# Linear attention and four experts on one core: w1 of expert 0 in halves of F by two row blocks, layer 1 of tile 0 split at two head pairs, a new order of the first steps, last stores on three queues

## The chip, the cores and the metric

The kernel runs on one core of a Trainium2 chip. The metric is the device time of one execution in microseconds. Times are medians over several executions; the profile is of one further execution. In the profile PE is TensorE (matrix products), PEld its weight loads, DVE is VectorE, ACT is ScalarE, POOL is GpSimd, and SP is SyncE, which mostly issues DMAs. A "q" behind the name means the queue that issues, not the engine's arithmetic.

## What is computed

```python
def phi(x):
    return np.where(x > 0, x, np.exp(x) - 1.0) + 1.0
q_p, k_p = (phi(q), phi(k))                      # (8, 8, 576, 64): batch, heads, sequence, head size
kv = np.einsum('bhsd,bhse->bhde', k_p, v)
z = np.sum(k_p, axis=2)
num = np.einsum('bhsd,bhde->bhse', q_p, kv)
den = np.einsum('bhsd,bhd->bhs', q_p, z)[..., None] + 1e-06
attn = num / den
x = attn.transpose(0, 2, 1, 3).reshape(4608, 512)
p = domain_probs / (domain_probs.sum(-1, keepdims=True) + 1e-09)
for e in range(4):                               # w1: (4, 512, 1024), w2: (4, 1024, 512)
    out += p[:, e:e + 1] * (np.maximum(x @ w1[e], 0.0) @ w2[e])
```

All arrays are float32.

## The kernel before

**Tiles.** The 4608 tokens are nine tiles of 512. Tiles 0 to 7 are the first 512 tokens of each of the eight batches, and tile 8 gathers the last 64 tokens of all batches. For each batch the kernel makes phi(k), phi(q), the matrix kv with z as a 65th column, the numerators and denominators, and turns the normalized result into `xT` (features on partitions, tokens along the row). Then four experts follow, each with a layer 1 (`w1`), a ReLU and a layer 2 (`w2`). Products are in float16 with float32 sums in PSUM.

**Two forms of the experts.** In tile 0, expert 0 uses plain products in layer 1, and all four experts use plain products in layer 2 (`y`). All else uses seven products in place of eight on 2 x 2 blocks. The blocks' sums come from DVE (sums of weights, steps `s` for w1 and `t` for w2), from POOL (sums of tokens `ts`, except in tile 0, where DVE makes them, and sums of hidden values `hs`), and from copies on ACT between the products.

**The names of the steps.** The order list uses these names, and so do the change and the prediction:

- `lq0..3`, `lk0..3`, `lv0..3`: SP's loads of batch 0. `lq` i holds half i//2 of the tokens and heads 0 to 3 or 4 to 7 (i % 2); `lk` and `lv` i hold two heads each. `lpr0` and `lpr` load the probabilities.
- `ke`, `kl`, `km`: exponential, linear part and their minimum of k in batch 0. `qe`, `ql`, `qm`: the same for q. `vc`: cast of v. `qT`: turn of q on TensorE and the copy out of PSUM. `kv` i: kv of head pair i and two copies. `nd` g h: numerators, denominators and normalization (`x_norm`) for the head pairs 2g and 2g+1 and token half h. `xT` i h: turn of x of pair i and half h, and its copy.
- `L` g h: layer 1 of expert 0 in tile 0, for columns 2g and 2g+1 of the eight column blocks of F and token half h. `CFG["CUT"][h][g]` says at which of the four row blocks (head pairs) it yields, so that other steps may stand between its parts. `warm` n: products on zeros.
- `w` l e r: piece r of the weights of layer l and expert e, a DMA that POOL issues and that casts to float16. `k`, `v`, `q` with a number and `rk`, `rv` among them: loads of batch 1, on POOL too.
- `p1..p7`, `c22`, followed by tile, expert and half: the seven products of layer 1 in block form with their copies. `y` e.nc: part c of layer 2 for 128 tokens n in tile 0. `m` j e.pi: product p of layer 2 in tile j, with i the row block of tokens.
- `b1.` and `b2.` steps: the attention of batches 1 and 2; `load` n is SP's load of a later piece of q, k or v.

**What sets the order.** The five engines' queues are written by hand. Each step has a position (`put_at`), and the steps are sorted by it. In front of the sorted list stands `CFG["EARLY"]`, the order up to tile 2's first products, in which a name stands once for each part of a step: the first time for its products, the next times for what follows them. Every instruction goes to its engine's queue in that order, so each engine works through its own steps in the order in which they stand in the list. `CFG` also says which engine makes a copy (`VC`, `QT`, `KC`, `XT`; A is ACT, V is DVE, P is POOL) and which PSUM bank a step uses (`BANK`).

**The end.** The last unit is tile 8 with expert 3. Its layer 2 uses four PSUM banks for the two row blocks, and its accumulators go out as soon as each is complete, by `store`, with two DMAs of 64 rows each, one for each of two queues. `L2ORD` is the order of the seven products of a unit, and the last unit has its own.

Of the kernel before, what the change touches and what calls it, by code (L numbers as in the profile page):

```python
# [77 lines left out]
    "VC": 'AAPA',  # L78
    "QL": 'VVPV',
    "QT": 'VVAV',  # L80
    "KC": ('VV', 'VA', 'AA', 'AV'),
    "XT": ('AA', 'VV', 'VA', 'VV'),
    "CUT": (((0, 3, 4), (0, 3, 4), (0, 4), (0, 4)), ((0, 2, 4),) * 4),
    "WARM": (14, 5, 3, 1, 2, 1, 1),
    "BANK": {'qT0': 'b', 'qT1': 'py', 'kv2': 'py', 'qT2': 'py', 'kv3': 'b', 'nd10': 'b', 'nd10+': 'py', 'nd00': 'py', 'xT20': 'b', 'nd01': 'b', 'xT00': 'b', 'xT10': 'py', 'xT30': 'py', 'nd11': 'b', 'L20': 'b', 'xT11': 'b', 'L30': 'e', 'L10': 'e', 'L11': 'e', 'L00': 'py', 'L31': 'b', 'L01': 'e', 'L21': 'py', 'b1.lk': 'py', 'b1.q1': 'py', 'b1.q3': 'b', 'b1.q0': 'py', 'b1.nd10': 'b', 'b1.qT0': 'py', 'b1.nd00': 'b', 'b1.xT0': 'b', 'b1.xT3': 'py', 'b1.qTl': 'py', 'b1.nl': 'py'},
    "EARLY": (
# [36 lines left out]
def kernel(  # L123
# [10 lines left out]
    nc = tc.nc  # L134
# [22 lines left out]
    NRAW = 6  # L157
# [57 lines left out]
    def load_w(layer, e, r):  # L215
# [5 lines left out]
        if layer == 2:  # L221
            fs = slice(r * 4, r * 4 + 4)
            nc.gpsimd.dma_start(out=w2_sb[e][:, fs], in_=w2_src[e, :, fs])
        elif e == 0:
            fs = slice(r * F // 4, (r + 1) * F // 4)
            nc.gpsimd.dma_start(out=w1_sb[e][:, :, fs], in_=w1_src[e, :, :, fs])
        else:
            ds = slice(r * 2, r * 2 + 2)
            nc.gpsimd.dma_start(out=w1_sb[e][:, ds], in_=w1_src[e, :, ds])
# [702 lines left out]
    def batch_steps(bt, nxt, put, at, at_next):  # L932
# [25 lines left out]
        for m, (n, i) in enumerate(mine):  # L958
# [5 lines left out]
            if not first:  # L964
                put(at[n][i] + 1, f"b{b}.load{m}", load, m + NRAW)
# [182 lines left out]
```

## Time and profile before

| | us |
|---|---|
| median of three runs (491.03 to 492.47) | 492.14 |
| the profiled execution: its time | 491.24 |
| the profiled execution: span of the program's instructions | 489.5 |
| TensorE busy | 477.5 (98%) |
| VectorE busy | 382.2 (78%) |
| GpSimd busy | 358.3 (73%) |
| ScalarE busy | 330.8 (68%) |
| first layer 1 product of tile 0 begins | 18.74 |
| DMAs of weights, 512 KB each as they land (x14), median from issue to landing | 10.7 |
| the four pieces of expert 0's w1, 256 KB each as they land, median | 6.1 |
| last add on VectorE begins, ends | 485.13, 485.61 |

A row of a list of groups or of the timeline gives start, duration, engine, line of the kernel, operation, the tiles written and read, their shapes and how many instructions were merged; in brackets stands the idle time of the engine before it and who ended it. The span is the time between the first and the last instruction that the profile shows, and the execution takes 1.7 us more. The granted clock of TensorE was 0.998 over the span.

### The profile page before, as it was taken

What the parts mean: (1) busy time and instruction counts of PE and PEld (TensorE: products, weight loads), DVE (VectorE), ACT (ScalarE), POOL (GpSimd) and SP (SyncE); (2) the same over time, 40 slices, a digit from 0 to 9 for tenths busy, and PEclk for the clock granted to TensorE, in tenths of its full rate; (3) what the DMA queues carried; (4) which work ended last, traced back from release to release, by engine and by line L of the source; (5) the groups of instructions that cost most, each with busy time, mean ns of one, the idle gap of its engine ahead of it and who ended that gap; (6) DMA issues with size and microseconds to landing.
All of it is one profiled execution on the core that took longest, in us unless ns stands there. A gap on an engine that the chain in (4) does not pass through costs nothing.

```text
span 489.5 us, 12007 instructions
## 1 busy us (share of the span) xinstructions
PE 477.5 (98%) x4567; PEld 407.8 (83%) x4567; DVE 382.2 (78%) x801; ACT 330.8 (68%) x656; POOL 358.3 (73%) x341
## 2 busy tenths in 40 slices
PE   7899998999999999999999999999999999999996
PEld 3676665898888988898889888988898888888885
DVE  5768999998958886788769885978687756775686
ACT  5489979855896498748884888478954565446530
POOL 4655044688967896789776976697769877987775
PEclk9999999999999999999999999999999999999999
DMA  8999968532445235524552345423131020002003
GB/s 280 199 226 262 249 127 243 154 94 47 134 154 122 50 112 190 113 60 113 171 128 65 95 144 145 92 56 119 56 76 28 5 95 1 2 0 88 2 1 86
DMA packets 81017, 53.67 MB, mean 110 GB/s; under 512 B 45152, under 2 KB 73696, under 8 KB 80960
## 3 DMA queue, kind: packets, MB, share of 16 engines
q1 hardware_dynamic: 70512, 41.05, 30.7%
q0 software_dynamic: 9888, 11.41, 12.3%
q8 instruction: 35, 0.57, 0.5%
q10 hardware_dynamic: 560, 0.46, 0.3%
q14 instruction: 22, 0.18, 0.1%
HBM read 45.16 MB, written 9.44 MB: 112 GB/s over the span
## 4 chain that ended last, share of the span: by engine, by line
PE 91%; ACT 3%; DVE 2%; DMA 1%; issue 1%; SPq 0%; DVEq 0%; ACTq 0%
PE py L809 39%; PE pb L866 24%; PE pe L866 18%; PE py L714 4%; PE ph L654 1%; PE psum_nd L471 1%; DMA kraws<-in_k_dram 1%; PE psum_kv L443 1%; DVE acc L705 1%; PE pb L809 1%; PE pe L809 0%; DVE t L761 0%; PE psum_nl L489 0%; ACT kp L343 0%; ACT u L877 0%
## 5 line engine op out<-in xcount | busy, mean ns | idle before, releaser
L705 DVE SCALAR_TENSOR_TENSOR acc<-py,p_sb,acc 128x256 f32<-128x256 f32 (+1 forms) x382 | 181.7, 488 | 43.1 <-PE py L809 37.3
L850 DVE CUSTOM_DVE_ANT_0 h<-pe,u 128x512 f16<-128x512 f32 x140 | 96.0, 687 | 46.8 <-PE pe L866 27.1
L866 PEld LDWEIGHTS <-w 128*128 128x128 f16 x1120 | 109.1, 98 | 17.4 <-issue 1.3
L776 POOL TENSOR_TENSOR hs<-h 128x512 f16<-128x512 f16 x64 | 73.9, 1154 | 59.4 <-DVE h L850 57.5
L809 PEld LDWEIGHTS <-h 128*128 128x128 f16 x1024 | 99.6, 98 | 12.7 <-issue 1.2
L809 PE MATMUL py<-w,h 128*128 128x256 f16 x744 | 106.4, 273 | 0.6 <-ACT acc L703 0.6
L877 ACT COPY u<-pb 128x512 f32<-128x512 f32 x140 | 82.5, 592 | 32.4 <-PE pb L866 29.7
L778 POOL TENSOR_TENSOR hs<-hs,h 128x512 f16<-128x512 f16 x64 | 75.0, 1173 | 26.4 <-PE py L809 24.0
L866 PEld LDWEIGHTS <-s 128*128 128x128 f16 x840 | 81.4, 98 | 12.1 <-issue 1.1
L866 PE MATMUL pb<-tt,w 128*128 128x256 f16 x560 | 83.7, 273 | 0.9 <-ACT u L877 0.9
L809 PEld LDWEIGHTS <-hs 128*128 128x128 f16 x768 | 74.4, 98 | 8.9 <-POOL hs L776 0.2
L782 POOL TENSOR_TENSOR hs<-h,hs 128x512 f16<-128x512 f16 x64 | 74.7, 1168 | 0.9 <-PE py L809 0.3
L780 POOL TENSOR_TENSOR h<-h 128x512 f16<-128x512 f16 x64 | 74.8, 1168 | 0.2
L809 PE MATMUL py<-t,hs 128*128 128x256 f16 x496 | 74.3, 273 | 0.0
L899 ACT ACTIVATE h<-pe 128x512 f16<-128x512 f32 x70 | 42.0, 600 | 44.1 <-PE pe L866 40.7
L892 ACT COPY pe<-pb 128x512 f32<-128x512 f32 x70 | 40.1, 574 | 38.6 <-PE pb L866 14.1
L920 ACT ACTIVATE h<-pb 128x512 f16<-128x512 f32 x70 | 42.0, 600 | 7.0 <-PE pb L866 7.0
L866 PE MATMUL pb<-tt,s 128*128 128x256 f16 x280 | 41.8, 272 | 0.6 <-ACT pe L892 0.6
L866 PE MATMUL pe<-tt,s 128*128 128x256 f16 x280 | 41.9, 273 | 0.0
L866 PE MATMUL pe<-xT,s 128*128 128x256 f16 x248 | 37.3, 273 | 0.0
L866 PE MATMUL pe<-xT,w 128*128 128x256 f16 x248 | 37.2, 273 | 0.0
L866 PE MATMUL pb<-xT,w 128*128 128x256 f16 x248 | 37.0, 273 | 0.0
(133 smaller groups left out, 598.7 us busy)
## 6 DMA issues: line engine op xcount, KB each, us to landing
out_dram<-acc SPq DMA_DIRECT2D x32, 256.0 KB, 2.5
w<-in_moe_w_dram POOLq DMA_DIRECT2D x14, 512.0 KB, 10.7
rawb<-in_k_dram SPq DMA_DIRECT2D x24, 256.0 KB, 3.3
rawb<-in_v_dram SPq DMA_DIRECT2D x24, 256.0 KB, 2.8
rawb<-in_q_dram SPq DMA_DIRECT2D x24, 256.0 KB, 2.7
rawq<-in_q_dram SPq DMA_DIRECT2D x4, 256.0 KB, 5.5
w<-in_moe_w_dram POOLq DMA_DIRECT2D x4, 256.0 KB, 6.1
rawb<-in_k_dram POOLq DMA_DIRECT2D x4, 256.0 KB, 8.6
```

Of the source, the lines that this page charges most:

```text
L705: nc.vector.scalar_tensor_tensor(out=acc, in0=ps, scalar=pscal, in1=acc, op0=AO.mult, op1=AO.add)
L776: nc.gpsimd.tensor_tensor(out=hs[0], in0=a21, in1=a22, op=AO.add)
L778: nc.gpsimd.tensor_tensor(out=hs[1], in0=hs[0], in1=a11, op=AO.subtract)
L780: nc.gpsimd.tensor_tensor(out=a21, in0=a11, in1=a21, op=AO.subtract)
L782: nc.gpsimd.tensor_tensor(out=hs[3], in0=a12, in1=hs[1], op=AO.subtract)
L809: nc.tensor.matmul(out=ps, lhsT=lhsT(k), rhs=rhs[:, k], start=first and k == 0, stop=k == FH - 1, skip_group_check=True,)
L850: nc.vector._custom_dve(TENSOR_ADD_SAT, out=out, in0=ps, in1=u, s0=BIG, s1=0.0)
L866: nc.tensor.matmul(out=ps[:, kk], lhsT=lk(kc), rhs=rhs[:, kc], start=first and kk == 0 and kc == 0, stop=kc == 1, skip_group_check=True,)
L877: nc.scalar.copy(u, self.b)
L892: nc.scalar.copy(self.e5, self.b)
L899: nc.scalar.activation(self.h[:, :, 0, 0:NH], self.e5, AF.Relu)
L920: nc.scalar.activation(self.h[:, :, 1, 0:NH], self.b, AF.Relu)
```

## The change

**Weights.** `w1` of expert 0 comes in four pieces of equal size as before. A piece was a quarter of F for all four row blocks; it is now a half of F (r // 2) for two row blocks (r % 2). Their order on POOL's queue goes from 3, 0, 2, 1 to 0, 2, 3, 1.

**Layer 1 of tile 0.** All eight halves `L` yield at two head pairs. Before, four of them yielded at three pairs or not at all.

**Engines and banks.** The v casts 0, 1 and 3 of batch 0 move from ACT to POOL, DVE and POOL, and cast 2 from POOL to ACT (`VC`). All turns of q are copied by ACT; most turns of x and most copies of kv are too. Warm-up products go from 27 in seven steps to 25 in five. The PSUM banks are dealt out anew.

**Order.** The whole list `EARLY` is new. Among others, SP loads the q of token half 1 first and `lq1` last, and the first two parts of many `L` steps stand ahead of the second two.

**Later steps.** In each batch from 2 on, the load behind q0 has its position moved from 1 to 2.8 behind q0. In the last unit product 5 stands ahead of product 6. `MOVE` sets the positions of five products: the first two products of the last unit for both row blocks (`m83.10`, `m83.11`, `m83.20`, `m83.21`) go to 512, which is ahead of `m82.40`; `m82.41` of the unit before goes to 528, which is behind product 6 of the last unit.

**Last stores.** The two halves of each store of the last unit went to SP and ACT, and those of product 7 and row block 1 both to POOL. Now those of product 7 go to SP and POOL (row block 0) and to ACT and POOL (row block 1), those of product 3 and row block 1 both to POOL, and the others to SP and ACT.

```diff
--- before.py
+++ after.py
@@ -75,46 +75,47 @@
     "LK": 'SSSS',
     "LV": 'SSSS',
     "KL": 'VVVV',
-    "VC": 'AAPA',
+    "VC": 'PVAP',
     "QL": 'VVPV',
-    "QT": 'VVAV',
-    "KC": ('VV', 'VA', 'AA', 'AV'),
-    "XT": ('AA', 'VV', 'VA', 'VV'),
-    "CUT": (((0, 3, 4), (0, 3, 4), (0, 4), (0, 4)), ((0, 2, 4),) * 4),
-    "WARM": (14, 5, 3, 1, 2, 1, 1),
-    "BANK": {'qT0': 'b', 'qT1': 'py', 'kv2': 'py', 'qT2': 'py', 'kv3': 'b', 'nd10': 'b', 'nd10+': 'py', 'nd00': 'py', 'xT20': 'b', 'nd01': 'b', 'xT00': 'b', 'xT10': 'py', 'xT30': 'py', 'nd11': 'b', 'L20': 'b', 'xT11': 'b', 'L30': 'e', 'L10': 'e', 'L11': 'e', 'L00': 'py', 'L31': 'b', 'L01': 'e', 'L21': 'py', 'b1.lk': 'py', 'b1.q1': 'py', 'b1.q3': 'b', 'b1.q0': 'py', 'b1.nd10': 'b', 'b1.qT0': 'py', 'b1.nd00': 'b', 'b1.xT0': 'b', 'b1.xT3': 'py', 'b1.qTl': 'py', 'b1.nl': 'py'},
+    "QT": 'AAAA',
+    "KC": ('AA', 'AV', 'VA', 'AA'),
+    "XT": ('AA', 'AA', 'AV', 'AV'),
+    "CUT": (((0, 2, 4),) * 4, ((0, 2, 4),) * 4),
+    "MOVE": {"m83.10": 512.0, "m83.11": 512.0, "m83.20": 512.0, "m83.21": 512.0, "m82.41": 528.0},
+    "WARM": (14, 3, 2, 1, 5),
+    "BANK": {'qT0': 'py', 'qT1': 'b', 'nd00': 'py', 'nd00+': 'b', 'kv2': 'py', 'xT00': 'b', 'kv3': 'b', 'nd10+': 'b', 'L00': 'b', 'L10': 'py', 'nd01': 'b', 'xT01': 'py', 'nd11+': 'b', 'L20': 'e', 'L30': 'e', 'L01': 'e', 'L11': 'py', 'L21': 'py', 'L31': 'b', 'b1.qT3': 'py', 'b1.nd30': 'py', 'b1.nd21': 'b', 'b1.q1': 'b', 'b1.qT1': 'py', 'b1.nd01': 'py', 'b1.xT2': 'b', 'b1.nd11': 'py', 'b1.xT0': 'b'},
     "EARLY": (
-        "lq0 lk3 lk1 ql0 qe0 lq2 ke1 ql2 kl1 w103 qe2 ke3 kl3 lv1 w100 lk0 lq1 km1 qm0 ke0 kl0 w102 w101 km3 warm0 qT0 ql1 lv0 qm2 km0 vc1 vc0 w111 lq3 ql3 qT0",
-        "warm1 kv1 kv1 lk2 qe3 lv2 vc2 kv1 qT2 qT2 lv3 rk1 kv0 w110 ke2 qe1 kv0 kv0 qm3 vc3 kl2 warm2 nd01 nd00 warm3 qT3 v0 nd00 w200 nd01 warm4 xT10 kv3 xT11",
-        "km2 kv2 kv2 qT3 xT11 xT10 kv2 xT01 kv3 w201 kv3 qm1 xT01 warm5 qT1 rk0 xT00 nd11 qT1 xT00 L01 rv1 nd10 nd11 warm6 xT31 nd10 rv0 L21 w120 xT21 L11 xT31",
-        "L31 xT21 L31 lpr0 L01 L31 xT20 xT20 k3 xT30 L11 w121 L01 v2 xT30 s0.0 L21 v1 L30 L11 L30 L20 L10 L21 p1.010 ts0.0 L20 p1.010 L00 ts0.2 b1.v0 L10 ts0.1",
-        "L10 s1.0 p1.011 s1.1 s1.3 s1.2 w210 p6.010 p1.011 k1 p2.010 L00 t0.0 p6.010 p6.011 p2.011 p2.010 p7.010 p5.010 q3 p2.011 p5.011 L00 y0.00 p6.011",
-        "p7.011 y0.01 p7.010 p7.011 y0.02 pr0 y0.03 y0.03 ts0.3 y0.30 c22.010 p4.011 p4.011 b1.lk c22.011 b1.lv p4.010 p4.010 s0.3 p3.010 y0.31 p3.011 y0.32",
-        "y0.33 k2 k0 y0.10 p1.020 p3.010 b1.k3 b1.lkm w211 p3.011 p1.021 y0.11 v3 s0.1 y0.20 w130 y0.12 y0.33 y0.13 p1.021 p2.021 p1.020 y0.21 y0.22 p2.020",
-        "s2.0 s2.1 s2.3 b1.v1 p2.021 y0.13 p2.020 p6.020 p6.021 p6.020 t0.3 s2.2 y0.23 p6.021 b1.km3 p5.020 p7.020 b1.v2 q2 y0.23 s0.2 y1.10 t1.0 p7.020",
...
-        "y2.03 ts1.0 b1.load4 b2.k0 p4.031 p4.031 b1.load1 p1.101 y2.30 p3.030 y2.23 p1.101 ts1.1 b2.lk c22.031 p3.031 y2.03 p1.100 b1.lqm y2.31 b1.qTl w231",
...
-        "y2.12 y2.13 b2.v0 p2.101 t3.0 b2.load5 p6.101 ts1.2 p7.100 y3.20 p7.100 b2.k3 y3.21 b2.v1 b2.load2 p5.100 p7.101 p7.101 b2.k1 b2.load3 y2.13 b1.nl",
...
+        "lq2 lq3 lq0 qe0 ql0 ql3 qm0 lk0 kl0 lk1 lpr0 ke0 km0 qe2 ql2 qm2 lv0 ke1 kl1 km1 warm0 qT0 lv1 lk2 qe3 qm3 warm1 qT2 qT0 vc0 w100 warm2 kv0 vc1 qT2",
+        "warm3 kv1 lk3 kv0 kv0 kl2 kv1 kl3 w102 kv1 nd01 lv3 nd01 warm4 xT11 xT01 ke2 km2 qT3 w103 vc3 lv2 ke3 vc2 nd00 w101 km3 xT01 w110 xT11 w111 kv3 k3 kv2",
+        "qT3 lq1 nd00 qe1 xT00 w200 kv3 rk1 ql1 kv3 kv2 w201 qm1 L01 kv2 nd11 xT10 L31 qT1 v0 nd11 rv0 xT00 xT10 L10 xT21 rk0 xT21 v1 xT31 L11 qT1 xT31 nd10",
+        "L01 L01 rv1 L31 w120 nd10 ts0.2 L00 ts0.0 xT30 ts0.1 xT20 L31 s0.0 L20 xT20 L30 xT30 L10 L10 L00 L00 L30 ts0.3 L30 p1.011 s1.0 p1.010 L11 L20 p1.010",
+        "p2.010 s1.1 L20 w121 p2.010 p1.011 L21 L21 L21 s1.2 p6.010 p5.010 w210 L11 s1.3 p6.011 y0.30 p2.011 p6.010 p7.010 w211 p7.010 s0.1 p6.011 c22.010 v2",
+        "y0.31 y0.00 p4.010 p2.011 y0.32 y0.33 p5.011 b1.k3 k0 pr0 y0.33 t0.0 t0.1 b1.km3 p7.011 p7.011 c22.011 y0.01 y0.02 y0.03 p4.010 b1.lk y0.20 y0.03 k2",
+        "p4.011 s0.2 p3.010 p4.011 p3.011 y0.21 y0.10 y0.22 p3.010 y0.11 b1.v0 q1 k1 p1.021 y0.23 p1.021 p3.011 p1.020 s2.0 y0.12 v3 p2.021 b1.lv p1.020 t0.3",
+        "s2.1 p2.020 s2.3 s2.2 y0.23 b1.v1 q0 t0.2 p6.020 p6.020 y0.13 p6.021 y0.13 y1.20 p7.020 y1.21 p2.020 p5.020 p7.020 w130 p2.021 y1.22 y1.23 t1.0 y1.10",
+        "w131 p5.021 b1.v2 q3 b1.lkm y1.11 p6.021 b1.k0 b1.k2 b1.k1 w220 t1.1 t1.2 p7.021 y1.12 p7.021 c22.020 p3.020 y1.23 b1.v3 b1.km0 p4.020 p4.020 y1.00",
...
+        "b1.xT1 p3.030 b1.nd21 y2.03 b1.xT0 b1.nd20 b1.nd21 y2.23 y2.10 y2.11 ts1.0 p1.101 p1.101 b1.load5 t1.3 b2.load0 t2.0 b1.xT2 y2.12 y2.13 b1.xT2 b2.k1",
+        "ts1.1 lpr y2.30 y2.31 p1.100 p1.100 y2.32 y2.33 p3.031 p2.101 y3.20 y2.13 b2.km1 p6.100 b2.lk p2.100 t3.0 b2.load4 p2.101 p6.101 p6.100 p2.100 b2.lv",
+        "ts1.2 p7.100 ts1.3 p7.100 b2.k0 y3.21 p5.100 y2.33 y3.22 t2.1 p4.100 y3.23 p6.101 p5.101 p4.100 p7.101 y3.30 c22.100 p3.100 b2.ones b1.qTl b2.v3 y3.00",
...
     ),
 }
 
@@ -222,8 +223,8 @@
             fs = slice(r * 4, r * 4 + 4)
             nc.gpsimd.dma_start(out=w2_sb[e][:, fs], in_=w2_src[e, :, fs])
         elif e == 0:
-            fs = slice(r * F // 4, (r + 1) * F // 4)
-            nc.gpsimd.dma_start(out=w1_sb[e][:, :, fs], in_=w1_src[e, :, :, fs])
+            fs, ds = slice(r // 2 * F // 2, (r // 2 + 1) * F // 2), slice(r % 2 * 2, r % 2 * 2 + 2)
+            nc.gpsimd.dma_start(out=w1_sb[e][:, ds, fs], in_=w1_src[e, :, ds, fs])
         else:
             ds = slice(r * 2, r * 2 + 2)
             nc.gpsimd.dma_start(out=w1_sb[e][:, ds], in_=w1_src[e, :, ds])
@@ -829,7 +830,8 @@
         if (j, e) == (NTILES - 1, E - 1):
             if p in (2, 3, 4, 7):
                 yield
-                store(j, ns, ds, *([(nc.gpsimd,) * 2] if (p, i) == (7, 1) else ()))
+                by = {(7, 0): "SP", (7, 1): "AP", (3, 1): "PP"}.get((p, i), "SA")
+                store(j, ns, ds, [on[x] for x in by])
         elif e == E - 1 and p in (3, 4):
             yield
             store(j, ns)
@@ -962,7 +964,7 @@
                 put(at[n][i], f"b{b}.{n}{i}", bt.phi_act, n, i)
                 put(at[n + "d"][i], f"b{b}.{n}m{i}", bt.phi_dve, n, i)
             if not first:
-                put(at[n][i] + 1, f"b{b}.load{m}", load, m + NRAW)
+                put(at[n][i] + (2.8 if (n, i) == ("q", 0) else 1), f"b{b}.load{m}", load, m + NRAW)
         put(at["lv"], f"b{b}.lv", bt.left_v)
         for n in "kq":
             put(at["l" + n], f"b{b}.l{n}", bt.left_act, n)
@@ -1072,7 +1074,7 @@
                     put_at(at + HSUM[d][i], f"hs{j}{e}.{d}{i}", hsum, d, i)
             order = L2ORD
             if n == len(units) - 1:
-                order, at = (1, 2, 6, 5, 7, 3, 4), at + NSLOT
+                order, at = (1, 2, 5, 6, 7, 3, 4), at + NSLOT
             for m in range(14):
                 put_at(at + L2AT[m], f"m{j}{e}.{order[m // 2]}{m % 2}", layer2_product, j, e, h, hss, order[m // 2], m % 2)
 
@@ -1097,6 +1099,7 @@
                     put(2 * NSLOT * E + CFG["TSUM"][i], f"ts{j + 1}.{i}", token_sum, j + 1, i)
                 else:
                     put(base + CFG["TSUM1"][i], f"ts1.{i}", token_sum, 1, i)
+        work = [(CFG["MOVE"].get(w[2], w[0]), *w[1:]) for w in work]
         work.sort(key=lambda w: w[0:2])
         live = {name: g for _, _, name, g in work}
         assert len(live) == len(work)
```

40 rows, old and new, of the table nl are left out of this document.

## The prediction

> **What bounds the kernel now.** I read the page first (share of each engine), then busy time by stretches, then TensorE's own timeline where a stretch is not full, and last the waits, which say what ended the gaps.
>
> ```profile
> span 489.5 us, 12007 instructions
> PE 477.5 (98%) x4567; PEld 407.8 (83%) x4567; DVE 382.2 (78%) x801; ACT 330.8 (68%) x656; POOL 358.3 (73%) x341
> ...
> 0.00:10.00 10.00, 7.25 (x23) 2.67 (x24) 4.81 (x11) 4.71 (x7) 3.56 (x11) 1.00 0.81 259
> 10.00:20.00 10.00, 7.66 (x138) 4.96 (x138) 8.69 (x25) 5.36 (x13) 8.50 (x12) 1.00 1.26 233
> 20.00:30.00 10.00, 10.00 (x96) 8.89 (x97) 7.14 (x18) 6.90 (x14) 4.12 (x6) 1.00 1.20 219
> ...
> 40.00:60.00 20.00, 20.00 (x181) 13.81 (x180) 16.48 (x30) 18.73 (x38) 5.11 (x7) 1.00 1.16 254
> 60.00:80.00 20.00, 19.12 (x152) 13.03 (x151) 18.91 (x36) 16.96 (x38) 5.81 (x7) 1.00 0.76 165
> 80.00:100.00 20.00, 19.33 (x190) 15.04 (x189) 18.77 (x31) 16.49 (x35) 14.40 (x11) 1.00 0.65 181
> ```
>
> The columns of a stretch are its length, then busy time of PE, PEld, DVE, ACT, POOL, the granted clock, DMA share, GB/s. TensorE is full from 20 us on, so the 98% leaves three places: the first 20 us, single stalls, and the end. The first 20 us are emptier than they look, since part of "busy" is warm-up on zeros:
>
> ```profile
> 1.19 5.77 PE L995 MATMUL warm_ps<-qz 128*128 128x512 f16 x14 [1.19 <-DVE qz L175]
> 8.49 0.40 PE L594 MATMUL psum_qT<-identh,qp 128*128 128x128 f16 x4 [1.53 <-DVE qp L586]
> ...
> 18.06 0.40 PE L594 MATMUL psum_qT<-identh,qp 128*128 128x128 f16 x4 [1.02 <-DVE qp L586]
> ...
> 18.74 0.60 PE L654 MATMUL ph<-xT,w 128*128 128x256 f16 x4
> ...
> 25.83 0.60 PE L866 MATMUL pb<-xT,w 128*128 128x256 f16 x4
> ```
>
> The first real layer 1 product starts at 18.74, and the first product of expert 1 at 25.83. By the order list, these pieces of real work stand ahead of it: 4 q turns of 0.21, 4 kv of 0.42, 4 x_norm of 0.36, 8 halves of xT of 0.13, and 54 layer 1 products of 0.109 (16 take 1.75 us in the chain): 10.9 us. So 25.83 - 10.9 = 14.9 us of the start carry no real work. The single stalls and the end:
>
> ```profile
> PE pb L866 <- ACT u L877: 0.9, 1, 0.9
> PE pb L866 <- ACT pe L892: 0.6, 1, 0.6
> PE py L809 <- ACT acc L703: 0.6, 1, 0.6
> ...
> 477.94 1.03 PE L809 MATMUL py<-t,h 128*128 128x256 f16 x8 [0.30 <-DVE acc L705]
> ...
> 480.84 5.88 SPq L692 DMA_DIRECT2D out_dram<-acc  x7
> 480.84 6.18 ACTq L692 DMA_DIRECT2D out_dram<-acc  x7
> 484.16 1.11 POOL L692 DMA_DIRECT2D out_dram<-acc  x2 [1.42 <-DVE acc L705]
> 484.69 0.92 DVE L705 SCALAR_TENSOR_TENSOR acc<-pb,p_sb,acc 128x256 f32<-128x256 f32 x2
> ```
>
> The last add ends at 485.6; SP and ACT are issuing stores until 486.7 and 487.0, and the span ends at 489.5. The profiled execution took 491.24 us, 1.7 more than its span; the median of the three runs is 492.14. Terms are worked out against 491.24 and taken off the median.
>
> **The start.** Before, each w1 piece of expert 0 holds all four row blocks of a quarter of F, and w1 lands late: issues at 9.4, 10.4, 11.2 and 12.0 with 5.4, 5.8, 6.3 and 7.9 us to landing give 14.8, 16.2, 17.5 and 19.9. Now w100 and w102 bring row blocks 0 and 1 for all of F, issued first, so every half split at two head pairs can begin with heads 0 to 3 alone, and the loads begin with their q. I follow the queues by rows. SP keeps its 13 loads, the probabilities now sixth; spaced like before (first at 3.6, last at 13.5), lq0 lands near 6.0, lk0 7.2, lk1 8.2, lv0 9.0, lv1 9.8, lk3 11.4. POOL does ql2 on the early q, then vc0 (0.93 by its vpos row) behind lv0, and only then issues w100, near 10.1 instead of 9.4; the landings are set by the full DMA stream rather than by that (the SP loads end at 13.5 either way), so I leave them.
>
> DVE: km0 to 8.3, qm2 8.9, kl1 and km1 9.8, qm3 10.2, vc1 10.7, kl2 11.1, kl3 11.9 (0.45 each), then kv1's copy 12.1. Behind that wait for lk3 stand x_norm and so TensorE. nd01 is at 12.1, its normalization (0.21 + 0.69) ends 13.5, xT01 and xT11 are copied by ACT to 14.5 (0.37 each, behind vc2); km2, km3 and nd00's normalization end 15.6, xT00 is turned, and L01's first four products start near 15.9, against 18.74. ACT takes all q turns and most xT and kv copies (+3 x 0.58, +2 x 0.21, +3 x 0.37) and has two v casts fewer (-2 x 0.66), 2.0 us more; it is busy 5.36 of 10 us there, which hides it. DVE, 8.69 of 10, gets 2.1 lighter (one v cast of 0.45 more; 3 x 0.42, 2 x 0.22 and 3 x 0.28 of copies less).
>
> Real work ahead of L01 is 3.4 us, so the empty part by then is 15.9 - 3.4 = 12.5. Next L01's second half needs w101, the fourth piece, which is issued behind vc3 on POOL: near 19.5 with 6.5 us of real work ahead, 13.0 empty. To be added are small gaps as before (0.2 to 0.3 behind warm-ups). I take 13.3: **1.6 us gained**. The two fewer warm-up products (0.4) are inside this. Bounds: 2.4 gained if w101 comes in time, 0.4 lost if L01 starts no earlier than 18.74 (18.74 - 3.4 = 15.3).
>
> One part of it is the piece itself: its rows are half of F instead of a quarter, with as many bytes. The stretch 14 to 18 us, quarters, moved 166 and 201 GB/s, and 20 to 26 us, longer rows, 198 to 228; by that a piece gets 0.1 us shorter, which is in the 19.5. The Trainium skill (DMA: Bandwidth & Descriptors, Specifications) puts line rate at 512 B and more, which a quarter row already has; by that the longer rows bring nothing, w101 lands near 19.9 and the gain is 1.2.
>
> **After the start.** Everything that follows comes sooner, while the weights don't. w200 lands at 27.9 and w201 at 30.4 (16.4 + 11.5, 17.1 + 13.3). Before, y0.30 had 18.1 us of real work ahead and the first use of w200 was at 31.0; now y0.30 has 14.6 ahead, so it comes at 27.9: cover gone, wait 0 to 0.5. y0.32 (17.2 ahead, 30.5) just meets w201, and y1.22 (29.4 ahead, 42.7) meets w211: that landed at 45.4 (36.7 + 8.7), and five 256 KB inputs (0.65 each) now queue behind it, so 42.2. I take 0 here; up to 1.6 is paid back if these weights come later.
>
> DVE is the next engine, 18.9 of 20 us in the stretch 60 to 80. There one of its weight sums took five times its usual 0.69 while POOL made token sums:
>
> ```profile
> 68.52 3.42 DVE L761 TENSOR_TENSOR t<-w 128x1024 f16<-128x1024 f16 x1
> ```
>
> That is 2.7 us of DVE, and the two PE stalls of 0.9 and 0.6, both on ACT, come 6 and 13 us behind it. In the new order t1.3, t2.0, t3.0 and t2.1 still stand among ts1.0 to ts1.3; t0.1, t0.2, t1.1 and t1.2 move forward into DVE's idle time before 45 us. I take 0, with 1.5 gained (both stalls go) and 1.5 lost (one such hit more).
>
> **Loads behind q0.** In each batch the load that follows q0 moves from 1 to 2.8 positions behind it on SP, past two output stores. In the stretch at 288 to 298 us the next accumulator's first write on ACT waited for such a store, the 0.6 us PE stall in the waits. Behind the moved load are one k load and the q transposes, 6 us later, and nobody waits for it within 20 us. 0 to 0.7 gained; I take **0.3**.
>
> **The end.** Four products of the last unit that need no hidden sums go ahead of m82.40, where TensorE stood 0.47 us (0.30 by DVE's accumulate); product 5 (first hidden sum) goes before 6 (second), and m82.41 becomes filler. DVE had 0.30 us idle there and then a pitch of 0.44 with no gap, so its last add comes **0.3** sooner. The stores: SP had five after 483.4 at 0.63 us each, so its last began at 486.17, 0.5 behind the last add, and ACT's last at 486.47; now each has four, POOL four instead of two (0.56 each, from 483.8 to 486.0). The last issues fall to about 0.1 behind the add: **0.4** more. Bounds: 0.9 gained, or 0.3 lost if POOL's stores start 0.3 late as at 484.16 and land last.
>
> **Sum**: 1.6 + 0.3 + 0.7 = 2.6 us. 491.24 becomes 488.6; on the median, 489.5.
>
> **The rivals.** *Paid back to the weights*: the start is faster, but PE meets w200, w201, w210 and w211 at their old landing times and waits out 1.6 us. For it: DMA share 1.16 to 1.26 all the way to 60 us. Against: by the sums above they land within 0.5 of need. 491.1, within 0.3%. The same time results if the start's chain slips, because ACT's first step now waits for the third load, so that the change doesn't do what it says there. Together 0.18.
> *Slower*: DVE's sums are caught by POOL's token sums more than once. ts1.0 to ts1.3 take 4.5 us of POOL; DVE has 1.1 of 20 us spare, so each further hit of 2.7 goes to PE nearly whole. It decides once PE pays over 4.1 us (2.6 and the 1.5 of the bound); two hits more give 492.14 - 2.6 + 5.4 = 494.9. Chance 0.13.
> *Cold TensorE*: the first 14 warm-up products ran at 0.41 us each (5.77 / 14), later ones at 0.22; fewer now fill the gaps, and if the clock fell back, 16 layer 1 products would take 1.7 us more: 491.2. The longest idle before was 1.53 with the clock at 1.00; by my replay the new ones are under 1. Chance 0.03. The Trainium skill (TensorE: Matmul & The Clock Gate, Part 1) has the clock halve after an idle window of about 3.4 us, by which this would not happen.
>
> **How the numbers follow.** 0.66 for the forecast. A measurement can tell about 0.3%, 1.5 us. Low end: 2.4 + 1.5 + 0.7 + 0.9 = 5.5 off, 486.6. High end: start's gain gone and one DVE hit more, less the end's 0.7, gives 492.9. Faster 0.66; within 0.3% 0.20, mostly the first and third rivals; slower 0.14.
>
> **What would show it.** Right: first L654 product at 15.5 to 16.5, first expert 1 product near 23.5; no DVE-bound gap near 478; last store issue within 0.2 of the last add. Wrong: PE waiting on DMA w at L714 between 27 and 45 us; L761 or L763 over 2 us more than once; a clock under 1.00 in the second stretch of 10 us; POOL's store landing last.

## The result and the profile after

| | before | changed |
|---|---|---|
| median us (range, runs) | 491.58 (490.87 to 492.47, 6) | 488.20 (487.52 to 489.46, 6) |
| profiled execution: time, span, us | 491.24, 489.5 | 487.91, 486.1 |

The ratio is 0.9937 [0.9925, 0.9950], so the kernel became 3.1 us faster (0.63% of 491.58; the two medians differ by 3.4). Gains in us below are such shares by the ratio, and the differences of the medians can be some tenths away from them. The forecast time was 489.5, from a median of three runs of 492.14; with all six runs the kernel before has 491.58, and that alone is 0.6 us of the 1.3 by which 488.20 lies below the forecast. Busy times of the engines and by stretches, of the changed kernel (columns as before):

```profile
span 486.1 us, 12014 instructions
PE 475.0 (98%) x4565; PEld 407.3 (84%) x4565; DVE 376.5 (77%) x794; ACT 332.4 (68%) x662; POOL 358.8 (74%) x344
...
0.00:10.00 10.00, 6.89 (x27) 2.61 (x27) 4.47 (x11) 4.23 (x7) 3.59 (x12) 1.00 0.75 247
10.00:20.00 10.00, 8.51 (x154) 6.46 (x153) 7.83 (x22) 6.67 (x18) 9.53 (x13) 1.00 1.15 243
...
40.00:60.00 20.00, 19.61 (x186) 13.57 (x184) 18.15 (x35) 19.42 (x40) 6.56 (x9) 1.00 1.17 256
60.00:80.00 20.00, 20.00 (x150) 13.19 (x149) 18.21 (x34) 17.41 (x36) 7.92 (x7) 1.00 0.77 181
80.00:100.00 20.00, 19.46 (x205) 16.16 (x204) 16.81 (x35) 17.22 (x39) 13.23 (x12) 1.00 0.62 176
```

TensorE's first number is the one to compare. It is fuller from 10 to 20 us (8.51 for 7.66), emptier from 40 to 60 (19.61 for 20.00), full from 60 to 80 (20.00 for 19.12). TensorE's timeline in the start, then its waits between 23 and 100 us, dates in the text:

```profile
7.97 0.40 PE L595 MATMUL psum_qT<-identh,qp 128*128 128x128 f16 x4 [1.47 <-DVE qp L587]
...
16.33 0.60 PE L655 MATMUL ph<-xT,w 128*128 128x256 f16 x4
...
23.16 1.06 PE L868 MATMUL pb<-xT,w 128*128 128x256 f16 x8
```

```profile
PE py L810 <- ACT acc L704: 0.5, 1, 0.5
PE pb L868 <- DVE s L747: 0.4, 1, 0.4
PE py L715 <- DMA w<-in_moe_w_dram: 0.2, 1, 0.2
```

Layer 1 starts at 16.33 and expert 1 at 23.16 (lines of the changed kernel are one or two higher: L654 is L655, L714 is L715, L866 is L868). The stalls of 0.9 and 0.6 us on ACT at 75 and 82 us are gone; in their place stand 0.2 at 30 us on a weight, 0.4 at 54 on a DVE sum behind weight w131, and 0.5 at 86. VectorE's weight sum in that place, which had taken 3.42 us, the next sum of its kind, and the POOL token sum that ran beside that one:

```profile
67.14 0.68 DVE L762 TENSOR_TENSOR t<-w 128x1024 f16<-128x1024 f16 x1
...
69.60 0.90 DVE L762 TENSOR_TENSOR t<-w 128x1024 f16<-128x1024 f16 x1
...
69.91 1.60 POOL L849 TENSOR_TENSOR tt<-xT,tt 128x512 f16<-128x512 f16 x1
```

The end, as the timeline has it (SP, POOL and ACT issue stores; DVE makes the last adds), and then the chain that ended last, from 478 us to the end (shares are of the window asked for, which differs by up to 4 us between the chains shown here and below):

```profile
479.08 2.86 SPq L693 DMA_DIRECT2D out_dram<-acc  x4
479.35 1.12 POOL L693 DMA_DIRECT2D out_dram<-acc  x2 [0.51 <-DVE acc L706]
479.53 2.68 ACTq L693 DMA_DIRECT2D out_dram<-acc  x4
480.32 0.92 DVE L706 SCALAR_TENSOR_TENSOR acc<-pb,p_sb,acc 128x256 f32<-128x256 f32 x2
480.66 1.05 POOL L693 DMA_DIRECT2D out_dram<-acc  x2 [0.19 <-issue]
```

```profile
by line: POOL out_dram L693 18.0%; POOL hs L783 12.8%; issue 7.9%; POOLq L1146 5.8%; POOLq L693 0.2%
```

The kernel before had, from 478 us on, a chain of products and adds, with no POOL in it:

```profile
by line: PE pb L809 21.9%; DVE acc L705 18.6%; PE pe L809 14.6%; PE py L809 8.6%; issue 0.2%
```

So the work that ends the span has moved from the products to POOL. The last add ends at 481.24 (480.32 + 0.92) instead of 485.61, 4.37 earlier, but the span only 3.4 earlier: 3.9 us lay behind the last add before (489.5 - 485.61), 4.9 lie there now. That 1.0 has two parts. The last store, on ACT, landed 2.87 us behind the last add before and 3.13 now. POOL's closing, the end of the long DRAIN that stands behind the stores in its queue (L1143 before, L1146 now), came 0.18 us behind that landing before (488.66 for 488.48) and 0.99 now (485.36 for 484.37). From there to the end it is 0.8 us in both.

Where the 3.4 us come from, in these two profiles. The second column counts, in us, how much less was empty or lost; "lost between products" is the distance of two products' starts beyond the usual 0.109.

| place | gained | how read |
|---|---|---|
| to the first expert 1 product | 2.0 | 25.83 to 23.16 is 2.67, less 0.66 of layer 1 work that now stands behind it |
| from there to batch 2's first kv product | 1.3 | that product comes 3.31 earlier (136.25 to 132.94), less 2.0 |
| the stall at 297 us | 0.5 | 0.73 lost between products before, 0.20 now |
| the gap at 478 us | 0.5 | 0.47 between products before, none now |
| behind the last add | -1.0 | 3.9 before, 4.9 now |

The terms add up to 3.3, and the spans differ by 3.4; the rest is rounding.

### The profile page after: what moved, and what is told of

Same layout as the page of the kernel before. It is cut to its first block, busy times and chain, and to the rows that moved or that the text cites. A ratio compares the mean times of both kernels' runs of the same rounds, so it can differ in the third digit from the quotient of the medians.

```text
span 486.1 us, 12014 instructions
## 1 busy us (share of the span) xinstructions
PE 475.0 (98%) x4565; PEld 407.3 (84%) x4565; DVE 376.5 (77%) x794; ACT 332.4 (68%) x662; POOL 358.8 (74%) x344
## 4 chain that ended last, share of the span: by engine, by line
PE 88%; DMA 6%; POOL 3%; issue 1%; SPq 1%; DVE 0%; POOLq 0%; ACT 0%; DVEq 0%
PE py L810 38%; PE pb L868 24%; PE pe L868 18%; DMA w<-in_moe_w_dram 5%; PE py L715 4%; PE psum_nd L472 1%; DMA vraws<-in_v_dram 1%; PE psum_kv L444 1%; POOL w L227 1%; POOL hs L783 0%; POOL hs L779 0%; POOL w L230 0%; PE psum_nl L490 0%; POOL out_dram L693 0%; POOL vpos L573 0%
## 5 line engine op out<-in xcount | busy, mean ns | idle before, releaser
L868 PEld LDWEIGHTS <-w 128*128 128x128 f16 x1120 | 108.9, 98 | 16.1
L779 POOL TENSOR_TENSOR hs<-hs,h 128x512 f16<-128x512 f16 x64 | 74.0, 1157 | 26.7 <-PE py L810 24.2
L868 PEld LDWEIGHTS <-s 128*128 128x128 f16 x840 | 81.2, 98 | 12.7 <-DVE s L747 0.9
L868 PE MATMUL pb<-tt,w 128*128 128x256 f16 x560 | 83.8, 273 | 0.0
L868 PE MATMUL pb<-tt,s 128*128 128x256 f16 x280 | 41.8, 273 | 0.4 <-DVE s L747 0.4
L868 PE MATMUL pe<-tt,s 128*128 128x256 f16 x280 | 42.0, 273 | 0.0
L868 PE MATMUL pe<-xT,s 128*128 128x256 f16 x248 | 37.1, 273 | 0.0
L868 PE MATMUL pb<-xT,w 128*128 128x256 f16 x248 | 37.1, 273 | 0.0
L868 PE MATMUL pe<-xT,w 128*128 128x256 f16 x248 | 37.0, 273 | 0.0
```

Of the source, the lines that this page charges most:

```text
L779: nc.gpsimd.tensor_tensor(out=hs[1], in0=hs[0], in1=a11, op=AO.subtract)
L868: nc.tensor.matmul(out=ps[:, kk], lhsT=lk(kc), rhs=rhs[:, kc], start=first and kk == 0 and kc == 0, stop=kc == 1, skip_group_check=True,)
```

## The experiments

The first theory was that the gain comes from the start alone and that POOL's stores give part of it back. The rivals: the start owes its gain to the order and not to the pieces; the products at the end, or the load behind q0, bring it; the stores are late because of their number, not because of POOL. Medians and ratios are against the kernel before on the same chip (490.98, 491.34 and 491.03 us, 17 to 25 runs, for the three groups).

### The changed kernel with the old last stores

```diff
-by = {(7, 0): "SP", (7, 1): "AP", (3, 1): "PP"}.get((p, i), "SA")
+by = {(7, 1): "PP"}.get((p, i), "SA")
```

> The changed kernel with the old choice of queues for the last stores (SP and ACT, and POOL for product 7 of row block 1 alone). Theory A, the prediction's: three queues save 0.4 us, so this takes 0.4 more than the changed kernel, 488.6 us. Theory B: a POOL store late in the list holds the end, because POOL closes about 1.6 us after its own last store has landed; then the end of the span moves from 4.9 us behind the last add (changed) back to 3.9 (before), and this takes 487.2. Theory C: the 64 KB writes crowd each other, on whichever queue; no change, 488.2.

Measured: 487.61 us (486.56 to 489.45), ratio 0.9932 [0.9911, 0.9953]. The span ends 3.85 us behind the last add, the changed kernel's 4.9. The chain at the end holds products and adds and no POOL. The time gained less than that 1.0 (0.6 us by medians), and the intervals overlap, so the time doesn't show it: in its profile TensorE waited 0.6 us more for pieces of w1, which the stores cannot have caused.

### The changed kernel with all last stores on SP and ACT

```diff
-by = {(7, 0): "SP", (7, 1): "AP", (3, 1): "PP"}.get((p, i), "SA")
+by = "SA"
```

> The changed kernel with all last stores on SP and ACT, none on POOL. Theory A: SP and ACT get six each behind product 7's add at 0.63 us, so the last issue is about 1 us behind the last add: 489.0 us. Theory B: POOL has nothing to close, the last landing alone sets the end, some 1.0 us ahead of the span's end: 3.9 to 4.2 us behind the last add, 487.3 to 487.6. Theory C: 488.2.

Measured: 488.21 us (486.80 to 489.05), 0.9938 [0.9918, 0.9958]. Without POOL the span ends 4.7 us behind the last add (481.55): the two queues' last issue begins 1.3 us behind it, lands at 484.90, and the span ends 1.3 behind that landing, where it was 1.0 before. Why this last part grew stays open. The times of this version, of the one above and of the changed kernel don't tell which is best. All fourteen profiles, those below among them, do: the six with two last stores on POOL end 3.80 to 3.86 us behind the last add, the seven with four 4.73 to 4.89, the one without 4.7. By the profiles neither no store on POOL nor four is right here, but two.

### The start alone, and the end alone

The start alone is the changed kernel with

```diff
-"MOVE": {"m83.10": 512.0, "m83.11": 512.0, "m83.20": 512.0, "m83.21": 512.0, "m82.41": 528.0},
+"MOVE": {},
...
-order, at = (1, 2, 5, 6, 7, 3, 4), at + NSLOT
+order, at = (1, 2, 6, 5, 7, 3, 4), at + NSLOT
```

and with the old stores and the old place of the load behind q0. The end alone is the kernel before with the moved products, their order and the new stores.

> The changed kernel with the whole end and the load behind q0 as before, so that only the start is changed (pieces of w1, splits, engines, banks, warm-ups, order). The prediction had 1.6 us for it, 490.0 against 491.6 before. By the two traces it is 2.0 in the first 23 us and 1.3 more up to 136 us: 488.3. Rival, paid back to the weights: 491.1. TensorE's first expert 1 product at 23.2 us in every case but a slip of the first chain.

> The kernel before with the new end alone: the moved products, product 5 ahead of 6 and the three queues; all else as before. The prediction had 0.7 us for it: 490.9 against 491.6. By theory B the products give 0.5 and the POOL stores take 1.0: 492.1. If the products give 0.5 and the stores nothing: 491.1.

Measured: the start alone 488.38 us (487.82 to 488.98), 0.9946 [0.9927, 0.9965], 2.65 us gained; the end alone 491.83 (490.64 to 493.12), 1.0015 [1.0002, 1.0028], 0.7 us lost. The end, for which the prediction had 0.7 gained, costs time. Together the two would give 1.9, and the whole change gave 3.1. The missing 1.2 is about what three intervals of 0.1 to 0.2% (0.6 to 0.9 us each) can leave, with the load behind q0 in neither of them. The profiles, one of each, agree with that: the start alone ends its span at 486.0 and the whole change at 486.1, and the table's other three terms (0.5, 0.5 and -1.0) sum to nothing.

### Quarters again, in the new order

```diff
-fs, ds = slice(r // 2 * F // 2, (r // 2 + 1) * F // 2), slice(r % 2 * 2, r % 2 * 2 + 2)
-nc.gpsimd.dma_start(out=w1_sb[e][:, ds, fs], in_=w1_src[e, :, ds, fs])
+fs = slice(r * F // 4, (r + 1) * F // 4)
+nc.gpsimd.dma_start(out=w1_sb[e][:, :, fs], in_=w1_src[e, :, :, fs])
```

> The changed kernel with w1 of expert 0 in quarters of F and all four row blocks, as before, in the new order of pieces (0, 2, 3, 1) and steps. Theory: the halves by row blocks make the early start possible. L10's first products need quarter 1 here, the fourth to land (19.1 to 19.9 us), and stand at 18.0 in the changed kernel, so PE waits 1.1 to 1.9 us there: 489.3 to 490.1 against 488.2. Rival: the new order alone does it, and the pieces give 0.1 us each by their longer rows at most: 488.2 to 488.6.

Measured: 489.33 us (488.68 to 493.89, 12 runs), 0.9966 [0.9946, 0.9986]; against the changed kernel's 0.9937 that is 1.4 us (the two intervals just touch), and its profile names 1.1 of them. TensorE's timeline in the start:

```profile
16.52 0.60 PE L655 MATMUL ph<-xT,w 128*128 128x256 f16 x4
...
18.32 0.61 PE L655 MATMUL ph<-xT,w 128*128 128x256 f16 x4 [0.62 <-DMA w<-in_moe_w_dram]
...
19.67 0.61 PE L655 MATMUL ph<-xT,w 128*128 128x256 f16 x4 [0.52 <-DMA w<-in_moe_w_dram]
```

Layer 1 starts as early as with halves (16.52), since the attention's order is the new one. Then each later column waits for its quarter, 0.62 and 0.52 us, 1.35 us apart. So of the start's gain the order brings the early first product, and the pieces keep TensorE fed afterwards: what counts, with the steps in this order, is which rows a piece holds. An order made for quarters was not run.

The halves landed at 15.18, 16.46, 17.79 and 19.06, 1.27 to 1.33 us apart, the quarters here 2.07, 1.33 and 1.35 us apart. So where nothing else came between, longer rows shorten a piece by less than 0.1 us, if at all. The rule of the Trainium skill (DMA: Bandwidth & Descriptors, Specifications), line rate from 512 B on, says none at all, and the runs can't tell these apart.

### The load behind q0 at its old place

```diff
-put(at[n][i] + (2.8 if (n, i) == ("q", 0) else 1), f"b{b}.load{m}", load, m + NRAW)
+put(at[n][i] + 1, f"b{b}.load{m}", load, m + NRAW)
```

> The changed kernel with the load behind q0 at 1 position behind it, as before, so ahead of the two stores on SP. The prediction had 0.3 us for this edit: 488.5 against 488.2, with one or two PE stalls of 0.5 to 0.7 us at the first accumulate on ACT between 190 and 300 us. Rival: the late stores come from other traffic, and the stall is there with either order: 488.2.

Measured: 488.63 us (487.55 to 489.85), 0.9941 [0.9920, 0.9963], the changed kernel's 0.9937 within its interval. The place can be read in the profiles. The stretch from 290 to 300 us, with the load at its old place and then in the changed kernel:

```profile
290.00:300.00 10.00, 9.56 (x89) 8.41 (x87) 6.12 (x13) 8.91 (x20) 6.36 (x7) 1.00 0.42 133
```

```profile
290.00:300.00 10.00, 9.96 (x92) 8.78 (x91) 6.23 (x12) 9.35 (x22) 6.86 (x7) 1.00 0.53 158
```

TensorE loses 0.44 us there with the load at its old place and 0.57 in the kernel before, on ACT's first write of an accumulator; with the load moved, it loses 0.04 here. Over all fourteen profiles, the seven with the load at its old place lose 0.20 to 0.59 us there in five cases and nothing in two, a mean of 0.30; the seven with the load moved lose 0.26 in one (the quarters), 0.04 in one and nothing in five, a mean of 0.04. On SP's queue, the kernel before and then the changed one:

```profile
291.76 0.39 SPq L318 DMA_DIRECT2D rawb<-in_v_dram  x1
293.19 0.81 SPq L686 DMA_DIRECT2D out_dram<-acc  x2
```

```profile
289.88 0.81 SPq L687 DMA_DIRECT2D out_dram<-acc  x2
290.78 1.98 SPq L319 DMA_DIRECT2D rawb<-in_v_dram  x1
```

The output stores no longer stand behind that load, and the accumulator mostly comes free in time. The move is worth about 0.3 us in this batch by the profiles. In another batch a like stall comes and goes by itself: at 244 us 0.3 are lost with the load at its old place, but also in the changed kernel's second profile, and none in its first. The time can't confirm 0.3 us, also because this profiled run waited 0.92 us for w1's last piece, which landed at 20.0 instead of 19.06.

### One warm-up product for each gap

```diff
-"WARM": (14, 3, 2, 1, 5),
+"WARM": (1, 1, 1, 1, 1),
```

> The changed kernel with 5 warm-up products (1, 1, 1, 1, 1) in place of 25; their output is used by nothing. If the clock of TensorE follows how busy it was, the first layer 1 products run at half speed (0.218 us instead of 0.109) for the first few us behind 16.3 us, and the granted clock is under 1.00 in the first 20 us: 1 to 2 us more, 489.2 to 490.2. If the warm-up products only fill gaps: 488.2 or a little less.

Measured: 488.94 us (487.77 to 489.89, 8 runs), 0.9949 [0.9930, 0.9967], 0.6 us over the changed kernel and within the intervals. TensorE's timeline, then the stretch of the same time:

```profile
7.28 0.61 PE L595 MATMUL psum_qT<-identh,qp 128*128 128x128 f16 x4 [5.48 <-DVE qp L587]
...
17.15 0.87 PE L655 MATMUL ph<-xT,w 128*128 128x256 f16 x4
...
18.30 0.60 PE L655 MATMUL ph<-xT,w 128*128 128x256 f16 x4
```

```profile
10.00:20.00 10.00, 9.02 (x135) 7.11 (x135) 7.15 (x20) 6.59 (x18) 8.49 (x12) 1.00 1.14 226
```

Four q turns take 0.61 us instead of 0.40, and of the first four layer 1 products three stand 0.21 us apart; from about 17.7 us all have the full pace of 0.109. Layer 1 starts 0.8 later (17.15). So a half pace exists and the warm-ups do avoid it at the first layer 1 products; its price here is about 0.6 us, which the time doesn't tell from none. The Trainium skill (TensorE: Matmul & The Clock Gate, Part 1) has the clock rise only after some 3.4 us of sustained work; the trace agrees, as the full pace comes 3.4 us after 14.35, from which on the products follow one another without a gap. The distance itself is no constant: in the changed kernel, whose 14 first warm-up products begin at 1.19, the full pace came at 5.5, 4.3 us later.

### The kernel before with one DVE sum moved ahead

```diff
-"y2.03 ts1.0 b1.load4 ...",
-"p1.100 p6.101 b1.qTl ts1.3 p3.031 b2.load0 y2.32 y2.33 b1.load3 t2.0 b2.lv ...",
+"y2.03 t2.0 ts1.0 b1.load4 ...",
+"p1.100 p6.101 b1.qTl ts1.3 p3.031 b2.load0 y2.32 y2.33 b1.load3 b2.lv ...",
```

> The kernel before with one edit: DVE's weight sum t2.0 stands ahead of POOL's token sums ts1.0 to ts1.3 in the order list instead of among them. Theory: the 3.42 us that t2.0 took there comes from POOL working at the same time, and the two PE stalls of 0.94 and 0.72 at 74 and 82 us come from it; t2.0 takes 0.7, both stalls go, 491.2 becomes 489.7. Rival: the stalls are ACT's own load (they end on ACT's copies) and stay, or another sum of DVE is caught instead: 491.2.

Measured: 490.51 us (489.39 to 491.58, 12 runs), 0.9978 [0.9963, 0.9993], 1.1 us gained by moving one step. Its DVE timeline and TensorE's waits from 60 to 100 us:

```profile
63.68 0.68 DVE L761 TENSOR_TENSOR t<-w 128x1024 f16<-128x1024 f16 x1
```

```profile
PE py L714 <- DMA w<-in_moe_w_dram: 0.8, 1, 0.8
PE pb L866 <- ACT pe L892: 0.2, 1, 0.2
```

Ahead of POOL's token sums the same sum takes 0.68 us instead of 3.42, the 0.9 us stall is gone and the 0.6 is 0.2. A new wait of 0.8 for a weight takes part of that in the profiled execution. That the long sum costs time, and stalls TensorE 6 us later by way of another engine, is thereby shown; the second stall shrank and did not go.

What made the sum long is less clear. It took 3.41 to 3.42 us in all four profiles that have the old order there, and in the kernel before it ran from POOL's issue of a weight load (68.30, 0.78 us) over the next two token sums (to 71.38). But the changed kernel's sum at 69.60 ran wholly beside token sums and took 0.90. So to stand among the token sums is not enough to be caught, and whether the issue or the exact moment of the start decides was not tested.

### The new stores alone, and the moved products alone

Both on the kernel before: its `store` call of the last unit replaced by the changed one; and `MOVE` with product 5 ahead of 6, the old stores kept.

> The kernel before with the new choice of queues for the last stores and nothing else. If POOL's later stores hold the end (it closes about 1.6 us after its last landing, and 0.8 more are left then), the end is 4.8 us behind the last add instead of 3.9: 0.9 more than before, 492.2 against 491.3. The prediction's term for the stores alone: 0.4 less, 490.9.

> The kernel before with the moved products and product 5 ahead of 6, and the old stores. TensorE's gap of 0.47 us ahead of m82.40 goes, and the last add comes 0.3 to 0.5 sooner: 490.8 to 491.0 against 491.3. If the stores' crowding takes it back: 491.3.

Measured: the stores alone 492.23 us (491.01 to 493.46, 12 runs), 1.0023 [1.0010, 1.0036], 1.1 us lost. The products alone 490.57 (489.87 to 490.89, 12 runs), 0.9983 [0.9973, 0.9992], 0.85 gained (0.46 by medians). Their sum, 0.3 lost, is near the end alone (0.7 lost) within the intervals. The chain at the end, stores alone and then products alone:

```profile
by line: POOL hs L782 17.8%; issue 17.2%; POOL out_dram L692 12.5%; POOL hs L778 8.8%; POOL hs L776 8.5%; POOLq L1144 3.9%; POOL h L780 0.5%; POOLq L782 0.3%; POOLq L692 0.1%
```

```profile
by line: PE pb L810 23.8%; PE pe L810 21.8%; PE py L810 7.3%; DVE acc L706 4.0%; issue 0.2%
```

With the new stores and nothing else, POOL holds the end. Its last two stores in that run, from the timeline:

```profile
485.07 1.04 POOL L692 DMA_DIRECT2D out_dram<-acc  x2 [0.19 <-issue]
```

They begin 0.9 us later than the kernel before's two on POOL (484.16). In all thirteen profiles with POOL in the last stores its closing comes 1.52 us (two stores) or 1.60 to 1.61 us (four) after its own last landing. In these four the span ends 0.75 to 0.85 after that:

| | POOL's last store landed | POOL closed | span ends |
|---|---|---|---|
| before | 487.14 | 488.66 | 489.5 |
| changed | 483.76 | 485.36 | 486.1 |
| old stores | 483.38 | 484.90 | 485.7 |
| stores alone | 488.11 | 489.72 | 490.5 |

That POOL waits for the landing is not shown. With no last store on POOL its DRAIN ended at 482.03, 2.9 us after its last sum (479.15), so a good part of the time behind the last instruction is there without any store.

### A better version, and the changed kernel again

Two changes to the changed kernel: POOL gets only one half of each store of product 7 and none of product 3's, and `L31`'s second half, whose rows land earlier, goes ahead of `L01`'s, which needs w1's last piece.

```diff
-"L01 L01 rv1 L31 w120 ...",
+"L31 L01 L01 rv1 w120 ...",
...
-by = {(7, 0): "SP", (7, 1): "AP", (3, 1): "PP"}.get((p, i), "SA")
+by = {(7, 0): "SP", (7, 1): "AP"}.get((p, i), "SA")
```

> The changed kernel with three stores fewer on POOL (the second halves of product 7 only, both row blocks) and with the second half of L31 ahead of that of L01, so that w101 has 0.44 us more time. The end should be 3.9 us behind the last add instead of 4.9, 0.6 to 0.9 less; and where w101 lands near 20 us, 0.4 less: 487.0 to 487.6 against 488.2. If landings and not POOL set the end: 488.0.

> The changed kernel as it is, on the same chip as the three others: 488.2. The wait ahead of L01's second half on w101 differs between runs (none to 0.9 us), by when w101 lands.

Measured: 487.38 us (486.68 to 488.50), 0.9917 [0.9900, 0.9934]; the changed kernel again 488.21 (487.53 to 490.20), 0.9940 [0.9920, 0.9960]. The better version ends 3.8 us behind its last add, with products and adds at the end of its chain, and no L655 product waits for a DMA:

```profile
by line: PE pb L810 14.7%; PE pe L810 7.3%; DVE acc L706 4.0%; PE py L810 0.9%; issue 0.2%
```

It is 0.8 us below the changed kernel by medians, 1.1 by ratios. The two intervals still overlap, so that it beats the changed kernel is likely and not shown; that it beats the kernel before is shown.

## Why the prediction was right, and where not

**The total was right, the split was not, and that is luck.** 2.6 us were forecast and 3.1 measured. The end cost 0.7 instead of bringing 0.7, while the start and what follows it brought more than the sum had.

**The start: right mechanism, size a little small.** L01 came at 16.33 (15.9 expected), expert 1 at 23.16 (23.5), so 12.9 us instead of 13.3 were empty: 2.0 gained, 1.6 expected. Two errors stand in this term. The first product came 0.4 later than expected; behind it the forecast had 0.8 more empty, 0.5 for w101 and 0.3 for small gaps, and there TensorE waited nowhere. w101, put near 19.5, landed at 19.06, in time. That is partly luck too: in the six profiles with this start w101 landed between 18.96 and 19.95, the wait for it was 0 to 0.9 us, and expert 1 began between 22.7 and 23.7. The quarters put 1.1 us of the term down to the pieces by their profile, 1.4 by the time.

**After the start: 0 expected, 1.3 found in the profile.** The forecast named the case as a bound: no DVE sum was caught in that profile, and both stalls went, 1.5 gained. The step that failed is the replay of t2.0: it still stands between ts1.0 and ts1.1 in the list, and I took this to mean that it would be caught as before. It isn't (0.68 us). Moving t2.0 alone shows that this place is worth 1.1 us ([0.3, 1.8] by its interval). A hit of 2.7 us on DVE thus cost TensorE 1.1 us by the time and 1.5 by the two stalls, and not nearly the whole, as the rival *Slower* had it. The weights did cost something: 0.2 at 30 us, and 0.4 at 54 behind w131. Idle time of TensorE over this part fell from 1.67 to 1.13 us, which is 0.5 of the 1.3; the remaining 0.8 lies in time in which the records show it busy in both kernels: by the distances of the starts, in many delays of under 0.2 us each. What makes them stays open.

**The load behind q0: 0.3 expected, 0.5 seen in this profile and about 0.3 over all**, at the place and by the mechanism that were named; the time could not tell it from none.

**The end: the products were a little under-sized, the stores had the wrong sign.** The moved products were put at 0.3, the idle time of DVE; 0.85 was measured alone ([0.4, 1.3] us by its interval, 0.46 by medians), and the gap of 0.47 in TensorE is gone. The stores were put at 0.4 gained and lost 1.1. The step that failed is taking the last issue for the end. By issues it came true: ACT's last one began 0.9 behind the last add before and 0.2 now (481.45 against 481.24). But the span ends with landings and with POOL's closing. SP's and ACT's stores from 478 us on took a median of 2.8 and 2.9 us to land (2.1 and 2.3 before), so the last of them landed at 484.37, 3.1 us behind the last add instead of 2.9, and the earlier issue was used up. POOL's closing at 485.36 then came a further 1.0 us behind that, where it had been 0.2. The bound "0.3 lost if POOL's stores start late and land last" had this case in sight, with too small a price: POOL's stores do not land last (483.76), and hold the end all the same.

**The rivals.** TensorE paid 0.2 at L715 and 0.4 behind w131 for weights, not 1.6. No DVE sum was caught by POOL in that profile; in the changed kernel's second one a sum at 86.60 took 1.52 us instead of 0.69 beside POOL's hidden sums, far from the 2.7 of the rival. The clock, once full, fell in no run before the last products. So none of the three took place, and the 0.66 stood on the right case, though for a sum in which two errors of about 1.5 us cancelled.

## What to carry to other kernels

At the end of a kernel, count a queue's end by what its engine does after its last landing, not by its last issue: read which engine holds the chain of the last microseconds, and deal the stores so that the queues close together. Here two stores on POOL did that, four made POOL late, and none made the other two queues late. When a first stage waits for weights, cut them by the rows that the first steps need, and test the pieces and the order apart. A sum of terms that comes out right can hide two wrong ones, so check each at its own place in the trace.

## What was not expected of the hardware

POOL closes 1.5 to 1.6 us after the landing of its own last store, in thirteen profiles. Twelve stores of 64 KB in the last microseconds took longer to land each when SP, ACT and POOL had four each (median 2.5 to 2.9 us) than with five, five and two (2.2 to 2.3, the old stores on the changed kernel). The granted clock column stood at 1.00 over a stretch in which products ran at half pace for most of it: the trace's first clock record in that run begins at 17.69 us, and the column counts the time before it as full. The start-to-start distance of products is the better witness. And the landing of the same weight piece varies by 1.0 us (18.96 to 19.95) between profiles of kernels that issue it alike.
